# Fused causal attention and gated FFN on one core: tile 0's output stores moved to the ACT queue, a fourth output buffer, and part of batch 1 issued three products earlier

## The chip, the cores and the metric

The kernel runs on one core of a Trainium2 chip. A core has a matrix engine, TensorE (PE; its weight loads are listed as PEld), three engines for everything else, VectorE (DVE), ScalarE (ACT) and GpSimd (POOL), and a fifth, SyncE (SP), that here only issues DMAs. Every engine works through its own list of instructions in order, and waits on semaphores for the others. ACT and POOL issue DMAs too, and such an issue stands in the engine's list like any other instruction.

The metric is the device time of one execution in microseconds (us). Before the change the median of 13 runs is 377.34 us (375.17 to 379.68).

## The reference

```python
# q, k, v: (8 batches, 8 heads, 576 positions, 64)
scores = q @ k.T / sqrt(64)                      # block-causal mask, blocks of 64
attn   = exp(scores - max) ; attn /= sum(attn)
x      = (attn @ v), heads side by side          # (8*576 = 4608 tokens, 512)
out    = (relu(x @ w_gate) * (x @ w_val)) @ w_out   # 512 -> 1536 -> 512
```

Inputs and output are float32; the kernel multiplies in bfloat16.

## The kernel before, in words

**FFN tiles.** The FFN is cut into nine tiles of 512 tokens: tiles 0 to 7 are the first 512 positions of each batch, tile 8 collects the last 64 positions of all batches (the "tails"). A generator, `ffn_gen`, yields after each matmul, called a product here, and a tile has 144 of them: 96 for gate and val (12 blocks of 128 hidden columns, 4 for gate and 4 for val each; L568), and 48 for the output (4 blocks `s` of 128 tokens, 12 products each; L625). Tile 0's output is split: for `s` = 0 and 1, the first 8 products are done early and copied to `ob` (L645), and the last 4 are added (L656). The remaining blocks are copied whole (L659).

**Attention.** It is done by visits `r` = 4 * batch + head pair. A visit computes scores (L378), takes exponentials on ACT (L387, L393), zeroes the masked corners on DVE (L686), multiplies with v (L491) and divides by the row sums on DVE (L456, L457). The result goes into `xT`, the FFN's input, by PE transposes (`to_xT_pe`, L537 and L538) for batches 0 and 1 and by DMA transposes (`to_xT_dma`, L543) from batch 2 on. The tails have scores at L412, exponentials at L424 and L433, products at L471, and go to `xTt` by DMA (L485).

**Order.** The order on PE, DVE, ACT, POOL and SP is that in which the Python code issues the work. Attention is laid between the FFN's products by lists of `(place, function)`: `run(base, events)` issues products up to `base + place` and then the function's work. Places count the products of all tiles on end, so tile 0 ends at 144, tile 1 at 288. `round_at` makes the events of one visit: begin, last exponential, corners, the products with v, and the transfer to `xT`.

**Inputs.** SP loads q, k and v of batches 0 to 3 as float32 into ten `stage` buffers (L120, L139, L149, L158); POOL casts them, a few are cast by ACT or DVE (L168, L178, L181, L189, L195). For batches 0 and 1 q and k are transposed on PE (`pe_mains`, L238, evacuated at L244) and `pe_tails` (L256, L262). For batches 2 and 3 they are transposed by DMA from SP (`transpose`, L209) and then put into order by DVE for q and POOL for k (`unpermute`, L223). From batch 4 on POOL loads with a cast (L276), and SP transposes (L286, L290).

**PSUM and buffers.** `ffnp` has three buffers of one bank, shared by FFN products, transposes and products with v; `sc` has two of two banks; `one` has one. `ob`, the output block in SBUF, has three buffers.

**Stores.** A block's store is not issued when its copy is made: the generator puts it into the list `store`, and issues it when the next block's copy has been issued (L661). `put` (L551) sends tile 0's stores out on SP's queue and those of tiles 1 to 7 on ACT's. So tile 0's fourth store is issued behind the copy of tile 1's first block, place 252. On SP it stands behind all that was issued before it there. In the built program, the DMAs of SP and ACT take eight completion semaphores in turn, and each DMA waits until the last one on the same semaphore has landed.

Of the kernel before, what the change touches and what calls it, by code (L numbers as in the profile page):

```python
# [10 lines left out]
FP = mybir.dt.float32  # L11
# [6 lines left out]
def kernel(  # L18
# [10 lines left out]
    nc = tc.nc  # L29
# [14 lines left out]
    sb = ctx.enter_context(tc.tile_pool(name="sb", bufs=1))  # L44
# [319 lines left out]
    def visit(r):  # L364

        b, hp = divmod(r, 4)
        at = attnT[r % 4]
        first = psum_sc.tile([128, 2, 512], FP, name="sc")
        second = psum_sc.tile([128, 2, 512], FP, name="sc")
        third = thirds()  # L370
        for c, hh in [(c, hh) for c in (2, 0, 1, 3) for hh in range(2)]:
            where = {
                0: first[:, hh, :],
                1: second[:, hh, 0:384],
                3: second[:, hh, 384:512],
                2: third[hh],
            }
            nc.tensor.matmul(  # L378
                where[c].rearrange("p (c n) -> p c n", n=128),
                kTm[b % 2][head_of(hh), c, hp, :],  # L380
                qTm[b % 2][head_of(hh), c:4, hp, :],
                start=True,
                stop=True,
            )

        def exp(sc, lo):
            return lambda: nc.scalar.activation(  # L387
                at[:, :, lo : lo + 512], sc, AF.Exp, scale=scale
            )

        def exp_third():
            for hh in range(2):
                nc.scalar.activation(  # L393
                    at[:, hh, 1024:1280], third[hh], AF.Exp, scale=scale
                )

        return exp_third, exp(first, 0), exp(second, 512)
# [44 lines left out]
    def corners(r, zero):  # L442

        at = attnT[r % 4]
        for lo, n in ((0, 512), (896, 128)):
            two = at[64:128, :, lo : lo + 2 * n].rearrange("p g (c n) -> p g c n", c=2)
            zero(two[:, :, :, 0:64])
# [52 lines left out]
    def head_av(r, hh):  # L500
        b, hp = divmod(r, 4)
        h = 2 * hp + hh
        at = attnT[r % 4]
        if hh == 0:
            xnats[r] = sb.tile([128, 4, 128], BF, name="xnat", bufs=3)
        xnat = xnats[r]
        if b > 0 or hh == 1:
            av = psum_ffn.tile([128, 4, 65], FP, name="ffnp")
        else:
            av = psum_one.tile([128, 4, 65], FP, name="one")  # L510
        products_with_v(b, h, at[:, hh, :], av)
        normalise(xnat[:, :, 64 * hh : 64 * hh + 64], av)

    def both_av(r):

        b, hp = divmod(r, 4)
        xnats[r] = sb.tile([128, 4, 128], BF, name="xnat", bufs=3)
        for hh in range(2):
            sc = psum_sc.tile([128, 2, 512], FP, name="sc")
            av = sc[:, 0, 0:260].rearrange("q (p e) -> q p e", e=65)  # L520
            products_with_v(b, 2 * hp + hh, attnT[r % 4][:, hh, :], av)
            normalise(xnats[r][:, :, 64 * hh : 64 * hh + 64], av)
# [26 lines left out]
    store = []  # L549

    def put(j, s, ob, n0, n1):  # L551
        if j < B:
            r0 = S * j + 128 * s
            (nc.sync if j == 0 else nc.scalar).dma_start(out[r0 : r0 + 128, :], ob)
        else:
            for i in range(2):
                r0 = S * (2 * s + i) + 512
                (nc.scalar, nc.sync)[i].dma_start(
                    out[r0 : r0 + 64, n0:n1], ob[64 * i : 64 * i + 64]
                )  # L560

    def ffn_gen():
        for j in range(B + 1):
# [67 lines left out]
                )  # L631

            def new_ob(n):
                return sb.tile([128, 512], FP, name="ob", bufs=3)[:, 0:n]

            part_sum = {}
            if j == 0:
                ops = [psum_ffn.tile([128, 512], FP, name="ffnp") for _ in range(2)]
                for f0 in (0, 4):
                    for s in range(2):  # L640
                        for f in range(f0, f0 + 4):
                            out_mm(ops[s], s, f, 0, 512, 0, 8)
                            if f == 7:
                                part_sum[s] = new_ob(512)
                                nc.vector.tensor_copy(part_sum[s], ops[s])  # L645
                            yield
            for s, n0, n1 in outs(j):
                op = psum_ffn.tile([128, 512], FP, name="ffnp")[:, 0 : n1 - n0]
                lo = 8 if s in part_sum else 0
                for f in range(lo, 12):  # L650
                    out_mm(op, s, f, n0, n1, lo, 12)
                    if f < 11:
                        yield
                if s in part_sum:
                    ob = part_sum[s]
                    nc.vector.tensor_tensor(out=ob, in0=ob, in1=op, op=AX.add)  # L656
                else:
                    ob = new_ob(n1 - n0)
                    nc.vector.tensor_copy(ob, op)  # L659
                if store:  # L660
                    store.pop()()  # L661
                store.append(lambda j=j, s=s, ob=ob, n=(n0, n1): put(j, s, ob, *n))
                yield
# [19 lines left out]
    dve, act, pool = nc.vector.tensor_copy, nc.scalar.copy, nc.gpsimd.tensor_copy  # L683
# [7 lines left out]
    with tc.manual_schedule(engines={E.PE, E.DVE, E.Activation, E.Pool, E.SP}):  # L691
# [57 lines left out]
        e1, e2 = Early(1), Early(2)  # L749
# [33 lines left out]
        def round_at(p, r, av, to_xT, after=(6, 13)):  # L783

            exps = []

            def begin():
                exps.extend(visit(r))
                exps[0]()
                exps[1]()  # L790

            return [
                (p, begin),
                (p + after[0], lambda: exps[2]()),
                (min(p + after[1], av[0] - 0.5), lambda: corners(r, zero_dve)),
                *(
                    [(av[0], lambda: both_av(r))]
                    if av[1] is None
                    else [(av[i], lambda i=i: head_av(r, i)) for i in range(2)]
                ),  # L800
                (to_xT[0], lambda: to_xT[1](r)),
            ]

        def tail_at(p, b, av):
            exps = []
            x = sb.tile([64, 512], BF, name="xtail", bufs=2)

            def begin():
                exps.extend(tail_visit(b))
                exps[0]()  # L810
                exps[1]()

            def end():
                tail_av(b, 1, x)
                tail_to_xT(b, x)

            return [
                (p, begin),
                (p + 6, lambda: exps[2]()),
                (av[0], lambda: tail_av(b, 0, x)),  # L820
                (av[1], end),
            ]
# [37 lines left out]
        def un(b, hp, engs=(dve, dve)):  # L860
            return lambda: early[b].unpermute(hp, engs)
# [6 lines left out]
        def mains_2(h0):  # L868
            e2.cast_qk(h0, 4, (pool, pool))
            e2.transpose(h0 // 4)  # L870

        def load_tails():
# [2 lines left out]
            e1.load_tails((2,))  # L875

        events = round_at(96, 4, (112, 112.1), (116, pe_xT), (6, 11))
        events += round_at(104, 5, (120, 120.1), (124, pe_xT), (6, 15))
        events += round_at(129, 6, (139, 140), (146, pe_xT), (4, 9))
        events += round_at(138, 7, (148, None), (153, pe_xT), (3, 8))  # L880
        events += [
            (80, lambda: e1.cast_qk(0, 4, (None, dve))),
            (93, lambda: e1.pe_mains(0, (dve, act))),
            (95, lambda: e1.pe_mains(1, (dve, act))),
            (120.2, lambda: e1.cast_qk(4, 4, (None, act))),
            (121, load_2),
            (125, lambda: e1.pe_mains(2, (dve, act))),
            (127, lambda: e1.pe_mains(3, (dve, act))),
            (133, lambda: mains_2(0)),
            (142, lambda: e0.pe_tails((dve, act))),  # L890
            (143, lambda: mains_2(4)),
# [3 lines left out]
        events = tail_at(24, 0, (40, 44)) + tail_at(116, 1, (132, 136))  # L895
        for r, p in ((8, 41), (9, 58), (10, 75), (11, 92)):
            events += round_at(p, r, (p + 21, p + 25), (p + 25, to_xT_dma))
        events += [
            (100, lambda: e1.pe_tails((dve, act))),
            (32, tails_2),  # L900
            (25, un(2, 0, (dve, pool))),
            (45, un(2, 1, (dve, pool))),
# [14 lines left out]
        for b in range(3, B):  # L917
            events = tail_at(120, b, (136, 140))
# [43 lines left out]
```

## Time and profile before

| | us |
|---|---|
| median of 13 runs | 377.34 |
| lowest, highest run | 375.17, 379.68 |
| the profiled execution's own time | 379.68 |
| its span, first to last instruction | 377.5 |
| PE busy | 362.2 (96%) |
| DVE, ACT, POOL busy | 171.7, 169.7, 112.0 |
| granted PE clock, mean | 0.986 |
| DVE waiting for `ob`'s stores (L659) | 6.6, in two waits, the longest 5.2 |
| PE waiting for a copy into `ob` | 3.6, once |
| PE waiting for POOL's `kTm` (L223) | 2.4, once |
| median landing of a 256 KB store from SP, from ACT | 5.2 (4 stores), 2.3 (28 stores) |

The profile covers one execution. Its rows give the engine, the line of the kernel, the operation, the tile written and the tiles read. A bracket such as `[1.14 <-DVE attnT L686]` says that the engine had been idle for 1.14 us and that the named instruction ended the wait. `SPq` and `ACTq` are DMA issues. PEclk is the share of full clock that PE was granted. Queues' packets can overlap, so a DMA share can exceed 1.

### The profile page before, as it was taken

The page shows a single profiled execution, that of the slowest core. Times are in us where ns is not written, and L with a number is a line of the kernel's source. Part 1 is how long each engine was busy: PE and PEld are TensorE (multiplying, and loading weights), DVE is VectorE, ACT ScalarE, POOL GpSimd, SP SyncE. Part 2 cuts the span into 40 slices and gives each one's busy share as a digit, 9 for nine tenths or more (in the row PEclk, how much of TensorE's full clock was granted, in tenths as well). Part 3 has the DMA queues.
Part 4 walks back from the last instruction along what each step waited for, and adds up shares of the span by engine and source line. Part 5 has one row for each costly group of instructions (what it writes and reads, how often), then busy time and mean ns, then how long its engine had stood idle before and what let it go on. Part 6 is the DMA issues. An engine that isn't in the chain of part 4 may idle for free.

```text
span 377.5 us, 7466 instructions
## 1 busy us (share of the span) xinstructions
PE 362.2 (96%) x2963; PEld 179.1 (47%) x2963; DVE 171.7 (45%) x398; ACT 169.7 (45%) x278; POOL 112.0 (30%) x142
## 2 busy tenths in 40 slices
PE   7999998979969999999999999999999999999996
PEld 2554454534534445544454445444544454444443
DVE  4744465436523554355425543454444534323332
ACT  4733755655504664455346533663266423302310
POOL 5675644276219950490039002100000000000000
PEclk9999999989978999999999999999999999999999
DMA  8999999949989999799649953947210130020004
GB/s 252 293 349 362 298 256 283 189 130 265 189 156 83 131 143 191 110 132 125 133 92 135 129 136 77 79 60 129 93 23 14 43 99 7 0 82 31 0 31 110
DMA packets 145187, 51.35 MB, mean 136 GB/s; under 512 B 124544, under 2 KB 139136, under 8 KB 145152
## 3 DMA queue, kind: packets, MB, share of 16 engines
q1 hardware_dynamic: 84192, 35.66, 43.2%
q0 software_dynamic: 56256, 7.08, 37.4%
q10 hardware_dynamic: 4704, 8.13, 6.6%
q8 instruction: 23, 0.38, 0.5%
q14 instruction: 12, 0.10, 0.1%
HBM read 37.75 MB, written 9.44 MB: 125 GB/s over the span
## 4 chain that ended last, share of the span: by engine, by line
PE 89%; DMA 4%; ACT 2%; DVE 2%; issue 1%; POOL 1%; SPq 0%; DVEq 0%; POOLq 0%; ACTq 0%
PE ffnp L568 50%; PE ffnp L625 23%; PE ffnp L491 4%; DMA out_dram<-ob 3%; PE sc L378 3%; PE ffnp L471 3%; PE one L378 1%; PE ffnp L238 1%; DMA stage<-in_q_dram 1%; PE sc L335 1%; PE sc L412 1%; ACT attnT L351 1%; POOL kTm L223 1%; ACT gate_sb L578 0%; PE sc L568 0%
## 5 line engine op out<-in xcount | busy, mean ns | idle before, releaser
L583 DVE TENSOR_TENSOR hT<-gate_sb,ffnp 128x512 bf16<-128x512 bf16 x106 | 72.8, 687 | 93.0 <-PE ffnp L568 75.7
L578 ACT ACTIVATE gate_sb<-ffnp 128x512 bf16<-128x512 f32 x108 | 64.8, 602 | 105.0 <-PE ffnp L568 101.4
L568 PE MATMUL ffnp<-xT,wg 128*128 128x512 bf16 x384 | 104.6, 382 | 0.4 <-ACT gate_sb L578 0.2
L625 PE MATMUL ffnp<-wo,hT 128*128 128x512 bf16 (+1 forms) x444 | 103.6, 378 | 0.3 <-DVE ob L645 0.2
L568 PE MATMUL ffnp<-xT,wv 128*128 128x512 bf16 x376 | 101.4, 382 | 0.0
L568 PEld LDWEIGHTS <-wg 128*128 128x128 bf16 x432 | 40.5, 98 | 48.0 <-issue 5.9
L568 PEld LDWEIGHTS <-wv 128*128 128x128 bf16 x432 | 40.2, 98 | 45.9 <-issue 3.0
L625 PEld LDWEIGHTS <-hT 128*128 128x128 bf16 x444 | 41.0, 99 | 42.7 <-issue 2.8
L387 ACT ACTIVATE attnT<-sc 128x1024 bf16<-128x1024 f32 x56 | 56.8, 1037 | 0.0
L659 DVE COPY ob<-ffnp 128x512 f32<-128x512 f32 (+1 forms) x35 | 23.7, 677 | 46.6 <-PE ffnp L625 40.0
L276 POOL DMA_DIRECT2D v_bf<-in_v_dram x20 | 16.9, 877 | 71.1 <-PE ffnp L471 52.0
L491 PEld LDWEIGHTS <-attnT 128*128 128x128 bf16 x640 | 26.5, 98 | 15.4 <-DVE xnat L457 3.3
L456 DVE RECIPROCAL recip<-ffnp 128x4 f32<-128x4 f32 (+1 forms) x73 | 13.0, 179 | 37.4 <-PE ffnp L491 25.9
L491 PE MATMUL ffnp<-v_bf,attnT 128*128 128x65 bf16 x570 | 26.7, 195 | 0.0
L393 ACT ACTIVATE attnT<-one 128x256 bf16<-128x256 f32 x28 | 10.7, 383 | 34.9 <-PE ffnp L378 30.9
L457 DVE TENSOR_TENSOR xnat<-ffnp,recip 128x256 bf16<-128x256 f32 x57 | 24.2, 425 | 2.0
L433 ACT ACTIVATE attnTt<-one 64x256 bf16<-64x256 f32 x8 | 3.0, 378 | 39.4 <-PE ffnp L412 39.4
L378 PEld LDWEIGHTS <-kTm 64*128 64x128 bf16 x224 | 9.5, 94 | 17.5 <-issue 10.4
L378 PE MATMUL sc<-qTm,kTm 64*128 64x512 bf16 (+1 forms) x168 | 17.2, 306 | 0.0
L471 PE MATMUL ffnp<-v_bf,attnTt 128*128 128x65 bf16 x320 | 12.8, 196 | 3.6 <-DVE ob L659 3.6
L471 PEld LDWEIGHTS <-attnTt 128*128 128x128 bf16 x320 | 12.2, 99 | 7.7 <-issue 3.9
L424 ACT ACTIVATE attnTt<-sc 128x1024 bf16<-128x1024 f32 x16 | 15.6, 1016 | 0.0
(86 smaller groups left out, 265.1 us busy)
## 6 DMA issues: line engine op xcount, KB each, us to landing
out_dram<-ob ACTq DMA_DIRECT2D x28, 256.0 KB, 2.3
stage<-in_moe_w_gate_dram SPq DMA_DIRECT2D x6, 512.0 KB, 9.1
stage<-in_moe_w_val_dram SPq DMA_DIRECT2D x6, 512.0 KB, 8.9
stage<-in_q_dram SPq DMA_DIRECT2D x6, 512.0 KB, 6.0
stage<-in_k_dram SPq DMA_DIRECT2D x6, 512.0 KB, 7.1
stage<-in_moe_w_out_dram SPq DMA_DIRECT2D x6, 512.0 KB, 9.2
stage<-in_v_dram SPq DMA_DIRECT2D x20, 128.0 KB, 5.5
stage<-in_v_dram SPq DMA_DIRECT2D x8, 256.0 KB, 6.9
```

The source lines that it names most:

```text
L276: nc.gpsimd.dma_start(dst, src[b, :, 128 * c : 128 * c + n, :].rearrange("h p d -> p h d"),)
L378: nc.tensor.matmul(where[c].rearrange("p (c n) -> p c n", n=128), kTm[b % 2][head_of(hh), c, hp, :], qTm[b % 2][head_of(hh), c:4, hp, :], ...
L387: return lambda: nc.scalar.activation(at[:, :, lo : lo + 512], sc, AF.Exp, scale=scale)
L424: return lambda: nc.scalar.activation(at[:, :, 2 * i : 2 * i + 2, 0:256], main[i].rearrange("p g (h n) -> p g h n", h=2), AF.Exp, scale=scale,
L457: nc.vector.tensor_tensor(out=out, in0=av[:, :, 0:64], in1=recip.to_broadcast([rows, n, 64]), op=AX.mult,)
L471: nc.tensor.matmul(av[:, i, :], attnTt[:, h % 2, lo + 64 * c : lo + 64 * c + 128], v_bf[b % 2][:, c, h, :], start=(i == 0 and c == 0), sto ...
L491: nc.tensor.matmul(av[:, p, :], at[:, col : col + 128], v_bf[b % 2][:, c, h, :], start=(p == 0), stop=(c == p), skip_group_check=True,)
L568: nc.tensor.matmul(to, (wg, wv)[t][f // 4][:, c, 128 * (f % 4) : 128 * (f % 4) + 128], x[:, c], start=(c == 0), stop=(c == 3),)
L578: nc.scalar.activation(gate_sb, gate, AF.Relu)
L583: nc.vector.tensor_tensor(out=h, in0=gate_sb, in1=val, op=AX.mult)
L625: nc.tensor.matmul(op, hT[f][:, 128 * s : 128 * (s + 1)], wo[f // 4][:, f % 4, n0:n1], start=(f == lo), stop=(f == hi - 1),)
L659: nc.vector.tensor_copy(ob, op)
```

## The change

Four edits. Tile 0's stores are issued on ACT like those of tiles 1 to 7. `ob` has four buffers instead of three. Tile 0's fourth store, which waits in the list, is issued at place 144 + 20 = 164. And in batch 1's second half, the transposes of head pairs 2 and 3 move from places 125 and 127 to 121.5 and 123, the begin of visit 6 from 129 to 126 and its products with v from 139 and 140 to 138 and 139, the begin of visit 7 from 138 to 137, while the transfer of visit 5 to `xT` moves back from 124 to 127. A place of 121.5 comes behind 121 products.

```diff
     def put(j, s, ob, n0, n1):
         if j < B:
             r0 = S * j + 128 * s
-            (nc.sync if j == 0 else nc.scalar).dma_start(out[r0 : r0 + 128, :], ob)
+            nc.scalar.dma_start(out[r0 : r0 + 128, :], ob)
...
             def new_ob(n):
-                return sb.tile([128, 512], FP, name="ob", bufs=3)[:, 0:n]
+                return sb.tile([128, 512], FP, name="ob", bufs=4)[:, 0:n]
...
         events = round_at(96, 4, (112, 112.1), (116, pe_xT), (6, 11))
-        events += round_at(104, 5, (120, 120.1), (124, pe_xT), (6, 15))
-        events += round_at(129, 6, (139, 140), (146, pe_xT), (4, 9))
-        events += round_at(138, 7, (148, None), (153, pe_xT), (3, 8))
+        events += round_at(104, 5, (120, 120.1), (127, pe_xT), (6, 15))
+        events += round_at(126, 6, (138, 139), (146, pe_xT), (4, 9))
+        events += round_at(137, 7, (148, None), (153, pe_xT), (3, 8))
...
-            (125, lambda: e1.pe_mains(2, (dve, act))),
-            (127, lambda: e1.pe_mains(3, (dve, act))),
+            (121.5, lambda: e1.pe_mains(2, (dve, act))),
+            (123, lambda: e1.pe_mains(3, (dve, act))),
...
         events += [
             (100, lambda: e1.pe_tails((dve, act))),
+            (20, lambda: store.pop()()),
             (32, tails_2),
```

## The prediction

> **What bounds the kernel now.** I read the page's busy shares first, then the list of waits, then the order of time around each long wait of TensorE, then the granted clock. TensorE (PE) is busy 96% of the span, so the only time to be had is where its row in the 40 slices drops, and whatever a drop costs afterwards.
>
> ```profile
> PE   7999998979969999999999999999999999999996
> PEclk9999999989978999999999999999999999999999
> DMA  8999999949989999799649953947210130020004
> ```
>
> One slice is 9.44 us. Behind the start PE drops at the 7th, 9th and 12th slices, and PEclk drops behind the last two of these. The windows cut around those two places show it (columns: length, busy time of each engine, PEclk, DMA share, GB/s):
>
> ```profile
> core 0: us, PE busy (x) PEld busy (x) DVE busy (x) ACT busy (x) POOL busy (x), PEclk, DMA share, GB/s
> ...
> 79.00:82.00 3.00, 0.61 (x9) 0.31 (x8) 0.92 (x2) 0.25 (x1) 2.55 (x4) 0.99 0.28 49
> 82.00:85.30 3.30, 3.30 (x21) 1.48 (x18) 0.61 (x2) 2.75 (x5) 2.93 (x3) 0.50 0.65 213
> ...
> 106.00:109.30 3.30, 0.89 (x5) 0.29 (x3) 0.00 (x0) 0.00 (x0) 0.00 (x0) 0.99 0.92 235
> 109.30:116.00 6.70, 5.52 (x31) 2.52 (x30) 2.59 (x7) 0.00 (x0) 4.36 (x5) 0.50 0.28 69
> 116.00:370.00 254.00, 253.98 (x2031) 123.62 (x2030) 113.03 (x256) 112.68 (x188) 50.62 (x61) 1.00 0.83 86
> ```
>
> After 116 us PE has no hole at all. Before it there are three waits; call them W1, W2 and W3. W1, order of time around 60 us:
>
> ```profile
> 54.60 0.68 SPq L554 DMA_DIRECT2D out_dram<-ob  x1
> ...
> 62.10 0.69 DVE L659 COPY ob<-ffnp 128x512 f32<-128x512 f32 x1 [1.44 <-DMA out_dram<-ob]
> 62.88 0.30 DVE L686 MEMSET attnT<- 64x128 uint32 x2
> ...
> 63.10 0.78 PE L491 MATMUL sc<-v_bf,attnT 128*128 128x65 bf16 x20 [1.14 <-DVE attnT L686]
> ```
>
> Tile 0's last copy into `ob` (s=3) waits until the first store has left its buffer; the corner memset is queued behind it on DVE, and the attention products wait for the memset: 1.14 us. W2:
>
> ```profile
> 74.12 0.63 SPq L158 DMA_DIRECT2D stage<-in_v_dram  x1
> ...
> 79.45 0.94 POOL L195 CAST v_bf<-stage 64x512 bf16<-64x512 f32 x1 [1.21 <-DVE hT L583]
> 80.35 1.03 POOL L223 COPY kTm<-perm 128x512 bf16<-128x512 bf16 x1
> ...
> 81.44 0.28 PE L378 MATMUL one<-qTm,kTm 64*128 64x256 bf16 x1 [2.39 <-POOL kTm L223]
> ```
>
> Here PE waits for a POOL copy that stands behind a cast whose load SP issued only at 74.12. W3:
>
> ```profile
> 104.52 1.30 SPq L554 DMA_DIRECT2D out_dram<-ob  x1
> ...
> 109.74 0.69 DVE L659 COPY ob<-ffnp 128x512 f32<-128x512 f32 x1 [5.16 <-DMA out_dram<-ob]
> ...
> 110.48 1.26 PE L471 MATMUL ffnp<-v_bf,attnTt 128*128 128x65 bf16 x20 [3.60 <-DVE ob L659]
> ```
>
> Tile 0's fourth store leaves SP only at 104.52, behind four transposes that SP issued from 98.96 on; tile 1's third copy needs its buffer. PE is idle for 3.60 us, and then runs at half clock until 116.07.
>
> **The change, part by part.**
>
> *W3: the fourth buffer and the early fourth store.* Tile 0 now holds four buffers of its own, and its fourth store goes out at product 164 (about 67 us in this trace) instead of behind product 252, so tile 1's copies find landed stores. The copy runs when DVE is free, 109.74 - 5.16 = 104.6, and PE goes on at 106.9. That gives back 3.60 us of idle time, and of the 5.59 us from 110.48 to 116.07 at clock 0.50, half: 2.8 us. Sum 6.4 us. What is late next: the transpose of batch 2's fourth head pair (L543), issued at 105.92 and landed at 110.1, which the fourth product of FFN tile 2 reads. Without W3 PE gets there at 106.9 plus 0.6 (the L471 group) plus 8 + 3 products of 0.216 (20 L568 products took 4.42 us, less than 0.22 each): 109.9. With the landing unchanged that costs 0.2; the SP store that stood before it is gone (104.52 to 105.92, 1.4 us), so it can as well cost nothing; ends 0 and 1.7 (with this landing later by what two stores take to move, 1.5 us, see W2). I take 0.2: **6.2 us**.
>
> *W1.* With its own buffer the copy starts when its product ends, about 61 us; the memset is done by 61.9, when PE arrives. 1.14 us go. But PE then reaches W2 1.14 us sooner, and W2 ends when POOL is done, not when PE arrives. Ends 0 and 1.14; by itself W1 is worth 0.
>
> *W2: does POOL's chain move?* Ahead of the load at 74.12, SP loses the store at 64.71, 0.57 us and about 0.09 to the next issue: up to 0.66 sooner (the store at 54.60 stood before loads that filled the queue: those four issues took 7.19 us; its 0.68 is covered by that). Against it, four stores of 256 KB now all move before W2's chain ends, where two did (54.60, 64.71): two more, in a stretch in which the DMA share is 0.94 to 1.25. One store took 0.66 to 0.80 us of the queue's landings (69.30 after 68.64; 62.01 after 61.20): up to 1.5 us later. Better than both: if the late v load (landed 79.4, 2.3 us behind the load issued just before it) was a chance delay, the chain ends 2.1 us sooner; 2.39 us of idle and the half-clock 1.7 us (3.4 us at 0.50) bound the gain at 4.1. Worse: 1.5 later, and a longer hole that holds the half clock for a second stretch, 1.7: 3.2 lost. The nearest rows are the 0.66 and the 1.5, of opposite sign and each an upper end; I take 0.
>
> *The clock.* The rows show 1.00 after W1's hole of 1.14 us, and 0.50 after W2's of 2.39 and W3's of 3.60; the sums go by that. [...]
>
> *Stores on ACT.* Four issues more on ACT; the 28 already there took 0.34 us each. The first stands between the copy that ends at 50.02 and the k cast at 50.07: it delays the cast to end at 51.5, and the transposes that read it start at 52.1 at the earliest (the two attention results that must leave PSUM first end at 51.52 and 52.07). If that cover were gone, 0.34. The second delays the exponentials of pair 7 by 0.34 - 0.21 = 0.13 us, covered by the copy and memset to 61.9. The third and fourth fit into ACT's idle 0.49 before 61.56 and 0.42 before 69.13. The real danger is a wait at the head of ACT: in the built program all DMAs of SP and ACT take eight semaphores in turn, and each waits for the landing of the eighth before it. For the four stores these landed, in this trace, at 50.05, 53.96, 58.09 and 64.30, and ACT gets to them at about 50.0, 57.6, 61.1 and 67.3: the first is a load that the next ACT instruction needs anyway, the others have 3 us in hand. Taken as 0.
>
> The store from SP at 54.60 landed after 7.41 us, those from ACT after a median of 2.3, which looks like a gain of 5 us each; but the ACT ones went out where the DMA share is lower, so I count none of it. [...]
>
> *Second half of batch 1 three products sooner.* The transposes (L238) move from products 125 and 127 to 121 and 123, the scores of pair 6 from 129 to 126, one PE transpose group from 124 to 127. PE then has 0.3 + 0.35 us of waiting for PSUM before the two L238 groups, and loses the 0.23 and 0.17 of now; the scores start near 54.1 with three products and one 0.24 us group still owed: 54.1 + 0.65 + 0.24 = 55.0, as before. Ends -0.4 and +0.7, ahead of W2, which swallows either: 0.
>
> **Sum.** -6.2 us. The profiled execution took 379.68 us for a span of 377.5, the slowest of the 13 runs, 2.3 above the median. From its own time the sum gives 373.5; from the median, 371.1. Part of its excess may be a half-clock stretch (1.7 us each) of the kind removed, so I add 0.5: **371.6 us**.
>
> **The rivals.**
> 1. *W2 shrinks too* (late load by chance, SP freed of its stores): POOL's chain 2.1 sooner, perhaps no half clock: 2 to 4 us more, about 368.5. For it: SP is the queue in front of that load. Against: PE arrives 1.14 sooner.
> 2. *W2 grows, or a new wait replaces W3* (the xT landing above): 2 to 3.2 us lost, 373.5 to 375. For it: the DMA share of 1.25 from 85 to 106 us.
> 3. *No measurable change*: W2 grows by about 6 us, eating W3's whole gain, 377.
> 4. *Slower*: ACT stands at the fourth store. If the eighth-earlier load lands later than 67.3 instead of 64.3, ACT's exponentials for the tail wait one for one, and PE behind them. The first 3 us cost nothing; it decides beyond 6.2 + 1.1 us more, a landing after 74.6; at 76 the time is 380. Against it: no load in that stretch took over 8.3 us to land.
>
> **How the numbers follow.** Forecast 0.62 (370 to 373.5), rival 1 0.15, rival 2 0.14, rival 3 0.04, rival 4 0.05. 0.3%, 1.1 us, is what a measurement of this kernel can tell from no change. Faster: 0.62 + 0.15 + 0.14 = 0.91, less 0.02 for the last of rival 2: 0.89; same 0.06; slower 0.05. The range reaches into rivals 1 and 2: 368.3 to 374.8.
>
> **What would show it.** Right: no DVE copy into `ob` waiting for a store; no L471 wait near 106 us and clock 1.00 there; the wait at L378 near 80 us still there, longer by about 1 us. Wrong: a long wait in front of an ACT store, PE waiting for L543's transpose at FFN tile 2, or the L378 wait past 5 us.

## The result, and the profile after

| | before | after |
|---|---|---|
| median, us | 377.58 (48 runs, 375.17 to 380.87) | 373.45 (11 runs, 371.82 to 375.95) |
| ratio, 95% interval | | 0.9891 [0.9871, 0.9911] |
| the profiled execution's own time, its span | 379.68, 377.5 | 373.25, 371.4 |
| mean granted clock in it | 0.986 | 0.995 |

The kernel became 4.1 us (1.1%) faster. A twelfth execution of after that is on record took 375.44 us and isn't in the median; with it the median would be 373.63. Between the two profiled executions the span is 6.1 us shorter, against a sum of 6.2.

The 40 slices of the kernel after, the rows that were shown of before:

```profile
PE   7999999979999999999999999999999999999996
PEclk9999999998999999999999999999999999999999
DMA  8999999949999999997499856956400420020014
```

The drops of PE at the 7th and 12th slices are gone. The one at the 9th (W2) is still there, and PEclk is below nine tenths in one slice only.

The windows around W2 and W3, of after (columns as before: length, busy time of PE, PEld, DVE, ACT, POOL, clock, DMA share, GB/s):

```profile
79.00:82.00 3.00, 0.44 (x7) 0.27 (x8) 1.08 (x2) 0.08 (x1) 3.00 (x5) 1.00 0.32 58
82.00:85.40 3.40, 3.35 (x23) 1.60 (x20) 0.61 (x2) 2.91 (x5) 3.09 (x4) 0.59 0.64 209
...
106.00:109.30 3.30, 3.30 (x44) 1.97 (x41) 1.57 (x5) 0.00 (x0) 1.51 (x2) 1.00 0.90 185
109.30:116.00 6.70, 6.70 (x87) 3.50 (x84) 4.10 (x6) 4.03 (x7) 6.70 (x9) 1.00 0.92 99
116.00:140.00 24.00, 24.00 (x197) 11.83 (x196) 12.56 (x32) 15.02 (x25) 17.46 (x21) 1.00 2.15 138
```

From 106 to 116 us PE was busy for 6.41 of 10.0 us before, part of it at half clock; now it is busy for all of it at clock 1.00. That is W3. The window from 79 to 82 is as empty as it was. The last line matters later: the DMA share from 116 to 140 us is 2.15.

W1's place in after, order of time, all engines:

```profile
61.05 0.34 ACTq L554 DMA_DIRECT2D out_dram<-ob  x1
...
61.25 0.69 DVE L659 COPY ob<-ffnp 128x512 f32<-128x512 f32 x1 [0.24 <-PE ffnp L625]
...
62.03 0.30 DVE L686 MEMSET attnT<- 64x128 uint32 x2
...
62.25 0.78 PE L491 MATMUL sc<-v_bf,attnT 128*128 128x65 bf16 x20
```

The copy now waits 0.24 us for its own product and for no store, and PE's attention products have no bracket: no wait. W2's place, the same view:

```profile
79.59 0.98 POOL L195 CAST v_bf<-stage 64x512 bf16<-64x512 f32 x1
...
80.52 1.03 POOL L223 COPY kTm<-perm 128x512 bf16<-128x512 bf16 x1
...
81.61 0.28 PE L378 MATMUL one<-qTm,kTm 64*128 64x256 bf16 x1 [2.56 <-POOL kTm L223]
```

POOL's copy starts at 80.52 (80.35 before) and PE goes on at 81.61 (81.44): the chain that ends W2 stands where it stood. PE's wait is 2.56 us instead of 2.39, and a wait of 0.72 us stands ahead of it at 73.00 us, for DVE, whose copy `qTm` had waited 2.9 us for a transpose of q to land. Together PE idles 0.9 us more there.

W3's place:

```profile
105.78 0.69 DVE L659 COPY ob<-ffnp 128x512 f32<-128x512 f32 x1 [0.88 <-PE ffnp L625]
...
107.05 0.77 PE L471 MATMUL ffnp<-v_bf,attnTt 128*128 128x65 bf16 x20
...
109.58 0.69 DVE L659 COPY ob<-ffnp 128x512 f32<-128x512 f32 x1 [1.10 <-PE ffnp L625]
```

Tile 1's copies wait for products only. The same group of L471 started at 110.48 behind 3.60 us of idle time.

**A ruler.** The groups of tail products (L471) stand at fixed places of the program, so the time from one to the next tells where a kernel lost time. Here are their starts in the profiled execution of each kernel that is spoken of below, in us; the group at place 184 comes before W2, that at 276 before W3, that at 309 behind it, 424 lies just ahead of FFN tile 3, 568 one tile on.

| kernel | 184 | 276 | 309 | 424 | 568 | 276 to 309 | 424 to 568 |
|---|---|---|---|---|---|---|---|
| before | 72.96 | 105.26 | 120.85 | 153.75 | 192.38 | 15.59 | 38.63 |
| after | 73.00 | 105.58 | 114.72 | 147.50 | 186.54 | 9.14 | 39.04 |
| e1_bufs | 72.52 | 105.04 | 114.17 | 147.16 | 189.60 | 9.13 | 42.44 |
| e2_act | 71.97 | 104.83 | 114.28 | 147.04 | 185.67 | 9.45 | 38.63 |
| e3_early | 73.11 | 105.03 | 114.16 | 146.93 | 186.55 | 9.13 | 39.62 |
| e6_w2 | 74.57 | 104.64 | 113.77 | 146.54 | 185.78 | 9.13 | 39.24 |
| e9_loads | 73.82 | 104.86 | 119.82 | 152.58 | 191.22 | 14.96 | 38.64 |
| e10_w2 | 73.31 | 103.08 | 115.97 | 148.76 | 187.39 | 12.89 | 38.63 |
| e11_both | 72.98 | 103.15 | 120.99 | 153.75 | 192.40 | 17.84 | 38.65 |
| e12_sp | 74.72 | 103.71 | 112.84 | 145.89 | 186.07 | 9.13 | 40.18 |

Undisturbed, 276 to 309 takes 9.13 us and 424 to 568 takes 38.63. From 568 to PE's last product it is 181.2 us in all of them but before (181.5). So before lost 6.46 us at W3, after loses 0.01 there, and after has 0.41 us between 424 and 568 that before has not. The sum of after against before: W3 -6.45, 184 to 276 +0.28, 424 to 568 +0.41, the rest -0.08: -5.84 at place 568.

### The profile page after: what moved, and what is told of

Read it like the earlier page. It is cut to its first block, busy times and chain, and to the rows that moved or that the text cites. A ratio compares the mean times of both kernels' runs of the same rounds, so it can differ in the third digit from the quotient of the medians.

```text
span 371.4 us, 7466 instructions
## 1 busy us (share of the span) xinstructions
PE 359.6 (97%) x2963; PEld 178.1 (48%) x2963; DVE 172.4 (46%) x398; ACT 169.6 (46%) x278; POOL 111.9 (30%) x142
## 4 chain that ended last, share of the span: by engine, by line
PE 75%; DMA 15%; SPq 4%; POOL 3%; issue 1%; DVE 1%; ACT 1%; POOLq 0%
PE ffnp L568 42%; PE ffnp L625 21%; DMA stage<-in_moe_w_val_dram 5%; PE ffnp L491 4%; DMA stage<-in_moe_w_out_dram 3%; DMA xT<-xnat 3%; PE sc L378 2%; DMA stage<-in_k_dram 2%; PE ffnp L471 2%; SPq L209 2%; DMA stage<-in_v_dram 2%; PE one L378 1%; DMA stage<-in_q_dram 1%; SPq L139 1%; SPq L158 1%
## 5 line engine op out<-in xcount | busy, mean ns | idle before, releaser
L625 PE MATMUL ffnp<-wo,hT 128*128 128x512 bf16 (+1 forms) x444 | 101.9, 374 | 0.3 <-DVE ob L645 0.2
L276 POOL DMA_DIRECT2D k_bf<-in_k_dram x16 | 14.4, 979 | 0.0
L276 POOL DMA_DIRECT2D q_bf<-in_q_dram x16 | 14.4, 948 | 0.0
```

Of the source, the lines that this page charges most:

```text
L276: nc.gpsimd.dma_start(dst, src[b, :, 128 * c : 128 * c + n, :].rearrange("h p d -> p h d"),)
L625: nc.tensor.matmul(op, hT[f][:, 128 * s : 128 * (s + 1)], wo[f // 4][:, f % 4, n0:n1], start=(f == lo), stop=(f == hi - 1),)
```

## The experiments

Ratios are to the kernel before, run on the same chip beside the experiments (median 377.95 of 15 runs for e1, e2, e3 and e5; 377.75 of 8 for e4, e6, e7 and e8; 378.25 of 24 for e9, e10 and e11; 378.19 of 11 for e12).

### Which edit carries the gain?

**e1_bufs**: before, with the fourth buffer alone.

```diff
-                return sb.tile([128, 512], FP, name="ob", bufs=3)[:, 0:n]
+                return sb.tile([128, 512], FP, name="ob", bufs=4)[:, 0:n]
```

> The kernel before with four output buffers and nothing else. Theory A (the wait for the fourth store's buffer near 106 us is the whole gain, and any edit that frees that buffer in time gets it): with four buffers tile 1's third copy no longer needs the buffer of tile 0's fourth store, so the wait of 3.6 us of TensorE and most of the half clock behind it go; tile 1's fourth copy needs that buffer now, a little after the store lands, so at most 1.5 us may be left. The first wait near 63 us goes as well. Time 373 to 375, ratio to before 0.990. Theory B (the gain comes from the ACT queue, which lands a store in 2 to 5 us where SP took 5 to 7, and from SP being rid of the stores): no gain, 377 to 378, as all stores stay on SP.

**e2_act**: before, with tile 0's stores on ACT alone.

```diff
-            (nc.sync if j == 0 else nc.scalar).dma_start(out[r0 : r0 + 128, :], ob)
+            nc.scalar.dma_start(out[r0 : r0 + 128, :], ob)
```

> The kernel before with tile 0's stores on ACT and nothing else: three buffers, the fourth store still issued behind product 252. Theory A: the store goes out on ACT right behind tile 1's first copy, near 99 us instead of 104.5, and lands near 102 us, ahead of the copy at 104.6; the wait near 106 us goes in full: 373.0 to 374.5. Theory B: the same time, 373 to 374.5. A third theory, C, that the early issue is needed: 376 to 378.

**e3_early**: before, with the fourth store issued early alone (on SP's queue, three buffers).

```diff
         events += [
             (100, lambda: e1.pe_tails((dve, act))),
+            (20, lambda: store.pop()()),
```

> The kernel before with the fourth store of tile 0 issued at product 164 and nothing else: on SP, three buffers. Theory A: it leaves SP before 75 us and has landed long before it is needed, so the wait near 106 us goes in full, while the first wait (1.14 us near 63 us) stays as before; that one is worth nothing, as TensorE waits for POOL near 81 us anyway. So the same time as the full change, 373.0 to 374.5. If the first wait is worth its 1.14 us: 374.5 to 375.5. Theory B: 377 to 378.

**e5_move**: before, with the moves in batch 1 alone.

```diff
-        events += round_at(104, 5, (120, 120.1), (124, pe_xT), (6, 15))
-        events += round_at(129, 6, (139, 140), (146, pe_xT), (4, 9))
-        events += round_at(138, 7, (148, None), (153, pe_xT), (3, 8))
+        events += round_at(104, 5, (120, 120.1), (127, pe_xT), (6, 15))
+        events += round_at(126, 6, (138, 139), (146, pe_xT), (4, 9))
+        events += round_at(137, 7, (148, None), (153, pe_xT), (3, 8))
...
-            (125, lambda: e1.pe_mains(2, (dve, act))),
-            (127, lambda: e1.pe_mains(3, (dve, act))),
+            (121.5, lambda: e1.pe_mains(2, (dve, act))),
+            (123, lambda: e1.pe_mains(3, (dve, act))),
```

> The kernel before with the second half of batch 1 three products sooner and nothing else. Theory A: no change beyond 0.5 us, 377 to 378, with the three waits near 63, 81 and 106 us as before. Rival D (the order of batch 1 carries the gain): 374 to 376.

**e4_nomove**: after, with those moves undone.

> The full change without the reordering of batch 1's second half: ACT stores, four buffers, early fourth store. Theory A: the same time as the full change, 373 to 374. Rival D (the reordering is needed so that the ACT stores don't delay batch 1): 375 or more.

| kernel | median, us | ratio, 95% interval |
|---|---|---|
| e1_bufs | 373.94 (6 runs) | 0.9900 [0.9858, 0.9942] |
| e2_act | 372.55 (4) | 0.9868 [0.9835, 0.9901] |
| e3_early | 372.91 (4) | 0.9866 [0.9832, 0.9901] |
| e5_move | 378.34 (10) | 1.0016 [0.9978, 1.0053] |
| e4_nomove | 373.64 (5) | 0.9890 [0.9851, 0.9929] |

Each of the three edits that concern `ob` gives the whole gain by itself; the three intervals and that of the change overlap. The gain is one wait, W3, and it has three ways out: another buffer (e1), a queue on which the fourth store leaves sooner (e2: issued at 97.16, landed at 100.66, where SP's issue of 104.52 landed at 109.65), or the issue at place 164 (e3: from SP, issued at 75.52, landed at 80.28). That ACT's queue as such brings something falls with e1 and e3, whose stores stay on SP, and that the moves bring something falls with e5 and e4.

e3 also tests what the prediction said of W1. Its three buffers leave W1 in, and W1 is longer than before. Order of time on PE, e3_early (the two places are two stretches):

```profile
63.25 0.78 PE L491 MATMUL sc<-v_bf,attnT 128*128 128x65 bf16 x20 [2.65 <-DVE attnT L686]
...
80.70 0.28 PE L378 MATMUL one<-qTm,kTm 64*128 64x256 bf16 x1 [1.50 <-POOL kTm L223]
```

W1 costs 2.65 us here and W2 1.50 instead of 2.39 to 2.56: PE comes later and waits less. At place 276 e3 is within 0.55 us of after (105.03 and 105.58) with W1 in it.

e5's profiled execution, the fastest of its ten, has the buffers of before and no W3. Its SP queue:

```profile
101.32 1.29 SPq L209 DMA_TRANSPOSE perm<-k_bf  x1
102.67 0.58 SPq L554 DMA_DIRECT2D out_dram<-ob  x1
```

The store left SP 1.85 us sooner than in the profiled execution of before and landed at 107.35 instead of 109.65; the copy into its buffer ran at 107.44, 0.09 us later, and PE did not stand. PE also came later: W2 was longer in this execution. PE of e5_move, order of time:

```profile
82.50 1.01 PE L568 MATMUL ffnp<-xT,wg 128*128 128x512 bf16 x2 [3.42 <-DVE hT L583]
```

So it stood at place 276 at 106.59, 1.33 us behind before. W3 has no fixed size: this execution with three buffers and a late store has none.

### Can W2 be had as well?

**e6_w2**: after, with POOL's casts of batch 1's tails behind the copies of the second head pair and the v copy (place 190.5 instead of 176), so that the cast that waits for a late load no longer stands before `kTm`.

```diff
         def tails_2():
             e2.cast_tails((pool, pool))
             e2.transpose_tails()
+
+        def tails_1():
             e1.cast_tails((pool, pool))
             e1.cast_v_tail(pool)
...
             (46, v_2),
+            (46.5, tails_1),
```

> The full change, and the casts of batch 1's tails moved on POOL behind the copy that TensorE waits for near 81 us (from place 176 to 190.5); nothing else. Theory A says that this wait (2.56 us of TensorE in the changed kernel, then a half-clock stretch worth 1.7 us) is there because that copy stands behind casts whose loads land late. It then goes, or shrinks below 1 us, and the clock stays at 1.00: up to 4.3 us less. Part may be given back at two later places where TensorE reads x transposed by DMA, near 108 and 150 us (0.2 us of waiting there in the changed kernel, 2.0 in the one with four buffers alone): 369.5 to 372. Rival: the copy waits for its own transposes, and nothing moves: 373 to 374.

**e7_w2_before** is the same edit of before, **e8_w2_early** that of e3_early.

> The kernel before with the same move of batch 1's tail casts on POOL, and nothing else. Theory A: the wait near 81 us goes, but the store that tile 1's third copy waits for still leaves SP near 104 us, so TensorE stands longer there, by about what it gained: 376 to 378. Rival (the waits are independent and their costs add): 373 to 374.

> The kernel before with the early fourth store (on SP, three buffers) and the move of batch 1's tail casts. The first wait, near 63 us (1.1 to 2.7 us), is left in; the second and third are out. Theory A: the first wait cost nothing only because the second hid it. With the second gone, it counts: 1 to 2 us more than the full change with the same move. Rival (it costs nothing in itself): the same time as that one.

| kernel | median, us | ratio, 95% interval |
|---|---|---|
| e6_w2 | 373.16 (4 runs) | 0.9874 [0.9831, 0.9916] |
| e7_w2_before | 373.28 (4) | 0.9886 [0.9861, 0.9911] |
| e8_w2_early | 373.64 (4) | 0.9901 [0.9871, 0.9930] |

e6 is no faster than after (373.45). The wait for POOL is gone, and another has come near it. DVE, POOL and PE of e6_w2, order of time:

```profile
78.23 2.56 DVE L223 COPY qTm<-perm 128x512 bf16<-128x512 bf16 x1
...
78.33 2.02 POOL L189 CAST v_bf<-stage 128x1024 bf16<-128x1024 f32 x2
...
81.44 0.59 PE L568 MATMUL ffnp<-xT,wg 128*128 128x512 bf16 x2 [1.21 <-DVE hT L583]
```

DVE's copy, 0.60 and 0.64 us as a median in before and after, takes 2.56 us while POOL's v casts run, the product `hT` stands behind it on DVE, and PE waits 1.21 us for the PSUM buffer that `hT` reads. PE is then at place 276 only 0.9 us ahead of after. But that is not all the new wait's doing: in this execution the q and k loads of batch 1 landed late (k at 51.75, in after at 50.62), PE stood 1.56 us for the k cast at 53.32, ahead of anything that the edit moves, ran at half clock from 54.48 to 57.90, and reached place 184 1.57 us behind after. From 184 to 276 e6 takes 30.07 us, after 32.58: 2.5 us of W2 are gained there.

e7 tells nothing of W2 alone: with the moved casts the buffers of `ob` fell differently in the built program, tile 1's third copy no longer follows the fourth store, and W3 was gone too (PE had no wait there, and one of 1.00 us at 110.08 for a transpose). It shows once more how little holds W3 in place. e8, with W1 still in it (2.55 us), had a wait of 1.80 us near 82; its ratio is 0.0027 (1.0 us) above that of e6, inside both intervals, so whether W1 counts once W2 is smaller is not decided.

Apart from e1 (374.4), the kernels without W3 end at spans of 370.5 to 371.8 us, with holes in different places. The column 424 to 568 shows a part of the reason; e1_bufs has it most clearly. Order of time on PE, e1_bufs:

```profile
152.48 0.38 PE L568 MATMUL ffnp<-xT,wg 128*128 128x512 bf16 x1 [2.00 <-DMA xT<-xnat]
```

And on SP's queue, e1_bufs:

```profile
133.52 7.77 SPq L286 DMA_TRANSPOSE kTm<-k_bf  x1
...
142.70 4.61 SPq L543 DMA_TRANSPOSE xT<-xnat  x3
```

FFN tile 3 needs `xT` of batch 3, whose transposes stand on SP behind batch 4's (one issue held SP for 7.77 us) and then land late, while POOL's loads of batch 4 move. Call it W4. In the profiled execution of before PE comes there at 156.7, and those transposes have landed by 154.3. In after PE waits 0.17 us there, in e3 0.82, in e6 0.36, in e1 2.00 and then runs a stretch at half clock. That made W4 my theory of the next floor: what is gained before 150 us is given back there.

### Where is the next floor?

**e9_loads**: after, with batch 4's first loads on POOL 22 products sooner, so that the transposes behind them come sooner.

```diff
+            (126, lambda: load_qkv(4, (0, 1))),
             (137, v_3),
...
                 for at, which in ((4, (0, 1)), (46, (2,))):
+                    if b == 3 and at == 4:
+                        continue
                     events.append((at, lambda b=b, w=which: load_qkv(b + 1, w)))
```

> The changed kernel with one move: batch 4's loads of its first two row blocks go out on POOL's queue 22 products sooner (ahead of the second half of batch 2's v copy), so that the DMA work of 116 to 140 us starts earlier. Theory (the next late thing is the transposes of x for batch 3, L543, landing at 150.6 to 152.2 us, which FFN tile 3 reads): PE has no wait at L568 near 152 us; since that wait was only 0.17 us in the changed kernel's profile, the time alone is within 0.8 us of the changed kernel, 372.5 to 373.7. Rival (the end at a span of 370.5 to 371.8 in every run so far is only the sum of TensorE's work, nothing is late at tile 3): no difference in the L543 landings, same time. Second rival: the earlier loads collide with the tails of batch 1 and the transpose that tile 2 reads at 110 us; then W2 is longer than 2.6 us or PE waits over 1 us near 110 us, and the time is 374 to 376.

**e10_w2**: e6_w2, with the copies of the second head pair asked for 7 products sooner, so that DVE's copy doesn't stand beside those casts.

```diff
-            (45, un(2, 1, (dve, pool))),
+            (38, un(2, 1, (dve, pool))),
```

> The changed kernel with W2 taken away on both of its engines: POOL's casts of the tails of batch 1 go behind its copy of kTm and its v copy, and the copies of batch 2's second head pair are asked for 7 products sooner, so that DVE's copy of qTm doesn't stand beside those casts. If W2 is a hole by itself, PE's wait of 2.56 us at 81.6 us and half of the 3.4 us at clock 0.50 go: 2.6 + 1.7 = 4.3 us, 369.1. If the transposes that FFN tile 3 reads (landing about 151 us) are the floor, PE gets there sooner and waits 1 to 3.5 us at L568 near 150 us, and the time is within 1.5 us of the changed kernel: 372 to 373.5. If the wait only moves again to another engine's copy near 81 us (over 1 us of PE idle there), the time is 372.5 to 373.5 without a wait at L568.

**e11_both**: the edits of e9 and e10 together.

> The two edits together: batch 4's first loads 22 products sooner, and W2 taken away on POOL and DVE. If FFN tile 3's transposes were the floor and the earlier loads lift it, the gain of W2 stays: 2 to 4 us under the changed kernel, 369 to 371, with no wait of PE over 0.5 us after 75 us. If the floor is elsewhere, it is as e10 within 0.8 us. If the earlier loads collide with the tails' landings, 374 or more.

| kernel | median, us | ratio, 95% interval |
|---|---|---|
| e9_loads | 376.93 (10 runs) | 0.9963 [0.9921, 1.0005] |
| e10_w2 | 373.84 (9) | 0.9880 [0.9842, 0.9917] |
| e11_both | 378.87 (10) | 1.0034 [1.0000, 1.0067] |

e9 is slower than after, by the two ratios by 2.7 us (0.9963 / 0.9891 = 1.0073), and the reason is that of the second rival, a little over its range of 374 to 376: the earlier loads met another transpose. There is no wait at 152 us, but that does not show W4 lifted: two of tile 3's transposes landed some 4 us sooner than in after (146.33 and 147.79 against 150.63 and 151.83), the third did not (152.53 against 152.20), and PE came there 5 us later (place 424 at 152.58 against 147.50). PE of e9_loads, order of time:

```profile
114.50 0.58 PE L568 MATMUL ffnp<-xT,wg 128*128 128x512 bf16 x1 [4.34 <-DMA xT<-xnat]
```

This is the transpose of batch 2's fourth head pair, which FFN tile 2 reads. SP issued it at 104.63, as in after (104.92); it landed at 114.46, after 9.83 us, where after's took 5.83. In e11 the wait is 6.33 us.

e10 is the answer on W2. Both waits near 80 us are gone: PE runs from 79 to 85 us with 5.99 of 6.00 us busy, and stands at place 276 2.5 us sooner than after, though it now idles 1.28 and 0.62 us ahead of that, at 73.31 and 75.12, behind DVE. But the time is that of after. The gain was given back, though not at W4. Order of time on PE, e10_w2:

```profile
110.40 0.38 PE L568 MATMUL ffnp<-xT,wg 128*128 128x512 bf16 x1 [2.02 <-DMA xT<-xnat]
```

And on SP's queue, e10_w2:

```profile
102.51 2.05 SPq L209 DMA_TRANSPOSE perm<-q_bf  x1
104.65 1.27 SPq L209 DMA_TRANSPOSE perm<-k_bf  x1
106.01 2.17 SPq L543 DMA_TRANSPOSE xT<-xnat  x1
```

PE comes to that product of FFN tile 2 at 108.4 and waits 2.02 us for the transpose that landed at 110.36, then runs 3.4 us at clock 0.50: 2.02 + 1.7 = 3.7, and the column 276 to 309 has 12.89 - 9.13 = 3.76. The next floor is this landing. The prediction had named it, as what is late next once W3 is gone; after just misses it (the transpose landed at 110.75 and PE read it at 110.81; in e2 PE waited 0.26 us).

**e12_sp**: e10_w2, with batch 3's second pair of transposes on SP behind that one.

```diff
-            (101, lambda: early[3].transpose(1)),
+            (117.5, lambda: early[3].transpose(1)),
...
-                events.append((2, un(3, 2, (dve, pool))))
+                events.append((12, un(3, 2, (dve, pool))))
```

> The kernel without W2 (e10_w2) with one change of order on SP's queue: the transposes of the second half of batch 3's q and k (L209), which nothing needs before FFN tile 3, go behind the transpose of batch 2's fourth head pair (L543), which FFN tile 2 reads; the copies out of them are asked for 10 products later. In e10_w2 SP issued that L543 at 106.01 us, behind 2.05 + 1.27 us of L209 transposes, it landed at 110.36, and PE waited 2.02 us and ran 3.4 us at clock 0.50: 3.7 us. Theory (that landing is the floor on which W2's gain was given back): L543 issued near 102.5, landed by 108, no PE wait at 110 us, clock 1.00 there, and 370.0 us (368.5 to 371.5), below both kernels. Rival (the next floor, FFN tile 3's transposes at about 150 us, is as near): the wait at 110 us is gone, PE waits 1.5 to 3.5 us at L568 near 148 to 151 us, 372 to 374. Second rival (the landing at 110 us is set by the DMA queue's load and not by its place on SP): it still lands after 109.5, 373 to 374.

Measured: 371.59 us (6 runs), ratio 0.9821 [0.9780, 0.9862], below both kernels: its interval ends under that of the change (0.9871). By the two ratios it is 0.9821 / 0.9891 = 0.993 of after, 2.6 us less, and 0.994 of e10, 2.2 us less, where the ends of the two intervals still overlap. On SP's queue, e12_sp:

```profile
100.03 5.15 SPq L543 DMA_TRANSPOSE xT<-xnat  x3
105.28 1.26 SPq L209 DMA_TRANSPOSE perm<-q_bf  x1
```

The transpose, the last of those three, left SP at 102.85 and landed at 107.14; PE had no wait there, and 276 to 309 is 9.13 again. So the order on SP set that landing, and a landing at 109.5 by load alone falls. PE of e12_sp, order of time, at FFN tile 2 and at tile 3:

```profile
108.94 0.39 PE L568 MATMUL ffnp<-xT,wg 128*128 128x512 bf16 x1
...
149.60 0.38 PE L568 MATMUL ffnp<-xT,wg 128*128 128x512 bf16 x1 [0.40 <-DMA xT<-xnat]
...
151.36 0.80 PE L568 MATMUL ffnp<-xT,wg 128*128 128x512 bf16 x2 [0.73 <-DMA xT<-xnat]
```

Now W4 does take part: 40.18 - 38.63 = 1.55 us at 150 us. The profiled execution is the slowest of e12's six; it also lost two holes at 51 to 54 us (1.06 and 1.54 us) and a stretch at half clock, because the q and k loads landed late there (k at 52.02, in after at 50.62). So both the theory (368.5 to 371.5) and its first rival (372 to 374) held in part.

## Why the prediction was right, and where it was off

Predicted was 371.6 us (368.3 to 374.8) and faster; measured 373.45.

**W3** was sized at 6.4 us, less 0.2 for the landing behind it. It measured 6.46 by the ruler, with 0.01 lost behind it. The clock's half of it (2.8 us) holds: 3.60 us of idle time alone would leave 2.9 of the 6.46 unexplained.

**W1** was counted at 0, because PE would wait longer at W2: the copy was to start about 61 and the memset to be done by 61.9 (measured 61.25 and 62.33). With W1 out, at place 276 PE is 0.3 us behind before, and e3, with W1 in, is no worse than after. Right.

**W2** was counted at 0 between -4.1 and +3.2, to be "longer by about 1 us". PE's release moved from 81.44 to 81.61, and PE idles 0.9 us more in two pieces. The size is right, in part by luck. The late v load left SP 1.36 us later than before (75.48 against 74.12), where the prediction had it up to 0.66 us sooner; but it took 4.05 us to land instead of 5.28, so it landed at 79.53 instead of 79.40. The transposes ahead of it landed later too, that of q at 71.73 against 70.20, which is the 0.72 us wait at 73.00, that of k at 72.64 against 71.29. That the four stores in front did this is not shown: in e1, whose stores leave SP as late as before, the transpose of k landed at 72.46 and the v load left at 75.27. Whether its late landing in before was chance stays open as well.

**Stores on ACT** at 0: each issue took 0.34 or 0.35 us, the first stood some 0.45 us at the head of ACT until the k load had landed (50.62, before 50.05), and the k cast ended at 52.15, 0.65 us later than the 51.5 that I had worked out; pair 6's scores still started at 54.48 (before 55.01, predicted 54.1). The first three stores from ACT, at 50.70, 55.84 and 61.05, took 5.01, 6.75 and 4.99 us to land (before, from SP at 54.60 and 64.71, 7.41 and 4.59): right not to count the difference in landing times as a gain. The landing times from the two queues lie in one range, and e1 and e3 gain as much with tile 0's stores on SP. In the traces of before and after the 176 DMA issues of SP and ACT are on eight semaphores, and none went out before the one ahead of it on its own had landed. The four stores of after went out 0.08, 1.59, 1.81 and 2.02 us behind those landings (50.62, 54.25, 59.24 and 65.33).

**The moves in batch 1** at 0, between -0.4 and +0.7: right (e5 1.0016, e4 as after).

**The step that was off** is the last of the sum: "Part of its excess may be a half-clock stretch [...] of the kind removed, so I add 0.5". From the profiled execution's own time the sum gave 373.5, and the profiled execution after took 373.25: for these two executions the sum was right. The median fell by 4.1 us (377.58 to 373.45) instead of 6.2, so this term, 0.5, should have been 2.1. Why the usual execution of before has 2.1 us less to lose stays open in part. A W3 that is smaller in most executions would explain it: e5 shows an execution with three buffers and no W3, and the half clock behind a hole varies too (two stretches behind 3.60 us in before, one behind 4.34 us in e9). But in the 58 runs of before beside the experiments, the 13 with a mean clock of 0.986 or less have a median of 378.8 us and the 20 with 0.994 or more one of 377.5. That is 1.2 us, where the two half-clock stretches that lie between 0.995 and 0.986 cost 3.4 us by themselves. So a run at the clock of the profiled one is not simply a usual run with W3 on top. How large W3 is in each of those runs no profile shows.

**"After 116 us PE has no hole at all"** was true of before and read as if it stayed so. PE comes to tile 3 some 6 us sooner, and 0.41 us is lost there in after, up to 3.8 in e1. This was left out of the list of what is late next, which went only as far as 110 us.

Of the rivals, the second (W2 grows or a new wait replaces W3, 373.5 to 375) names the place where the gain of a further edit goes, as e10 shows; in after itself that wait is not there. The first (W2 shrinks), the third (W2 eats the whole gain) and the fourth (ACT stands) did not happen.

## What to carry to other kernels

Before a wait is priced from one profiled execution, ask how far that execution lies above the median, and whether the wait could be what put it there: a wait that depends on a landing had no fixed size here (W3: 3.60 us in the execution of before, none in that of e5). When several edits each remove the same wait, only one of them is paid. And behind every removed wait go on along the busy engine's whole list, not only to the next transfer: here two transposes on one in-order queue, 40 us apart, were the next two floors, and taking out the next hole brought nothing (e10) until that queue was put in another order (e12).

## What the runs showed of the hardware that I had not expected

- From 45 us to the end of PE's work the half clock came in stretches of 3.413 us, or twice that (81.94 to 85.35 and 109.24 to 116.07 in before, 82.63 to 86.04 in after). They began within the hole (that of W3 in before, 106.88 to 110.48) or up to 1.2 us behind it: 1.02 us behind a hole that ended at 81.61 us in after, 1.02 us behind one of 2.02 us that ended at 110.40 in e10 (111.42 to 114.84). Length alone didn't decide: a hole of 2.65 us (e3 at 63 us, clock 1.00 from 62 to 70) and two of 1.66 and 1.93 (e9, at 74 and 82) cost no clock, while one of 1.56 us in e6 (at 53.32) was followed by clock 0.50 from 54.48 to 57.90. In before and after the stretches began whole steps of 3.413 us apart: in before at 81.94, 109.24 and 378.90, 8 and 79 steps, in after at 82.63 and 372.76, 85 steps. Counted from these starts, the full-clock steps between 45 and 365 us in which PE idled 2.39 and 2.36 us (before) and 2.39 us (after) were followed by half clock; all others had 1.14 us or less, and none of them was. The stretch of twice the length had 1.24 us of idle time in its first step. That is read from these two traces; no run shifted a hole to test what decides.
- DVE's copy of `perm` to `qTm` (128x512 bf16) took 0.60 us as a median in before (8 copies, 0.58 to 0.90) and 2.56 us in e6 at 78.23, where POOL's v casts ran from 78.33 to 80.35; the copy ended at 80.79. In before, where the copy began 0.12 us ahead of a POOL cast (at 79.33), it took 0.58 us, and the cast took 0.94 us, where the others of this form in before took 0.61. No run here separated the overlap of the two engines from other causes.
- A transpose of one and the same form, issued within 0.3 us of the same time from the same queue, landed after 5.83 us in after and after 9.83 us in e9, where POOL had issued loads of batch 4 from 103.09 us on; in after the first of them left at 111.34.
